# Linear attention and a leaky-ReLU feed-forward on one core: another threading of the first two batches

## The chip, the cores and the metric

The kernel runs on one core of one Trainium2 chip. The metric is device time in microseconds (us) of one execution. The time before is the median of three runs.

Engines are named as in the profile: PE is TensorE's matrix products and PEld its weight loads, DVE is VectorE, ACT is ScalarE, POOL is GpSimd, SP is SyncE, whose queue issues nearly all loads and stores. Each engine, and each queue, works through its instructions in the order of the program.

## The reference

Eight batches of eight heads, 576 positions, head size 64, go through linear attention with cosine and sine weights; the result, reshaped to 4608 rows of 512, goes through a feed-forward of width 2048.

```python
B, H, S, D = q.shape                      # 8, 8, 576, 64
theta = np.pi / 2.0 * pos / S
r = np.maximum(x, 0.0)                    # phi, for q and for k
phi = np.concatenate([r * c, r * s], axis=-1)
kv = np.einsum('bhsf,bhsd->bhfd', k_p, v)
z = np.sum(k_p, axis=2)
num = np.einsum('bhsf,bhfd->bhsd', q_p, kv)
den = np.einsum('bhsf,bhf->bhs', q_p, z)[..., None] + 1e-06
attn = num / den
x = attn.transpose(0, 2, 1, 3).reshape(B * S, H * D)
h = x @ w_in                              # 512 -> 2048
out = np.maximum(0.01 * h, h) @ w_out     # 2048 -> 512
```

## The kernel before

**Groups.** There are nine groups g of 512 rows: one for the first 512 positions of each batch, and a last one for the 64 tail positions of all eight. A group is handled as four tiles j of 128 positions. The order of all instructions is written out by hand; each engine keeps it.

**The stages of a group.** `q_prep` (L300) makes the cosine and sine halves of phi(q) for one tile, in f16 (`phi_half`: on VectorE a tensor_scalar, on ScalarE an activation with Relu). `q_transpose` (L324) turns the eight heads of a tile on TensorE and copies the result `qpT` out of PSUM. `k_main` and `v_main` prepare k and v for a range of heads, on engines named in the call; `k_tail` and `v_tail` do the 64 tail positions. `kv_half` multiplies k and v for four heads, first the two of one pair, then the two of the next, and ScalarE copies the sum out (L291). `num_half` makes numerators and denominators of two tiles and four heads, and `divide` on VectorE forms the quotient in three instructions (L350, L354, L355). `x_transpose_half` turns the quotients and ScalarE copies them into `xT`, the input of the feed-forward. `ffn1` makes two of the 16 blocks of the hidden layer in one PSUM tile (four chunks c of 128 model columns each) and ScalarE applies the leaky ReLU. `ffn2` sums 16 blocks into an output tile, four at a time (`part`), and `ffn2_out` copies it out and stores it.

**Threading.** While the feed-forward products of group g run on TensorE, the attention stages of the next groups are put between them. `weave` takes the units of feed-forward work with a position each, and steps with positions of their own; a step is issued ahead of the first unit at or past its position. Groups 0 and 1 are threaded by hand, ahead of the large weave at the end; from the third batch on `q_steps`, `kv_steps` and `out_steps` place the steps.

**Weights.** w_in comes in eight loads of 512 KB (`load_w1`, two chunks of 128 rows by 512 columns each) and GpSimd casts them to f16 (`cast_w1`). w_out comes in four quarters of 1 MB (`load_w2`) and VectorE casts them (`cast_w2`). `idle(n)` issues n products of zeros on TensorE.

**Loads in order on SP's queue.** First batch: q in two halves of heads, the tails of k and v, then k and v by halves; w_in; then w_out's first two quarters, q of the second batch, its tails, w_out's last two quarters, k and v of the second batch by halves, and q, k, v of the third. Staging tiles rotate through seven buffers.

**PSUM.** Pools "h" and "o" have two buffers each, "n" has one of two banks. A tile of a pool waits until the one that had its buffer before has been read.

Of the kernel before, what the change touches and what calls it, by code (L numbers as in the profile page):

```python
# [18 lines left out]
def kernel(  # L19
# [96 lines left out]
    def load_halves(b):  # L116
# [4 lines left out]

    w1 = [
        [const.tile([P, 2, 512], dt.float16, name=f"w1_{i}_{cp}") for cp in range(2)]
        for i in range(DFF // 512)
    ]
    w2 = const.tile([P, NFT, DM], dt.float16, name="w2")
# [5 lines left out]

    def load_w1(i, cp):

        if cp == 0:
            st["w1", i] = stage.tile([P, NKC, 512], dt.float32, name="w1st", tag="stage")
        sl = slice(2 * cp, 2 * cp + 2)
        nc.sync.dma_start(st["w1", i][:, sl], w1v[:, sl, 512 * i : 512 * (i + 1)])  # L138
# [10 lines left out]
    load_halves(0)  # L149
    for i in range(NB):  # L150
        for cp in range(2):
            load_w1(i, cp)

# [94 lines left out]
    def v_main(b, lo, hi, eng):  # L248
        copy(eng, vmain[b % 2][:, lo:hi, :, 0:D], st["v", b][:, lo:hi])
# [49 lines left out]

    def q_prep(g, j, lo=0, hi=H):  # L300
        src, c, _ = q_src(g, j)
        if lo == 0:
            st["qp", g, j] = qppool.tile([P, H, F], dt.float16, name="qp", tag="qp")
        qp = st["qp", g, j]
        phi_half(DVE, qp[:, lo:hi, 0:D], src[:, lo:hi], cos_t[:, c : c + 1])
        phi_half(DVE, qp[:, lo:hi, D:F], src[:, lo:hi], sin_t[:, c : c + 1])

# [57 lines left out]

    def num_half(g, jp, hg, where):

        if hg == 0:
            st["xp", g, jp] = qppool.tile([P, 2, H, D], dt.float16, name="xp", tag="qp")
        ps = psum(where, [P, 2, 512], dt.float32, "ps_numh")  # L370
        for o in range(2):
            for hh in range(4):
                h = 4 * hg + hh
                nc.tensor.matmul(  # L374
                    ps[:, o, hh * NE : (hh + 1) * NE],
                    lhsT=st["qpT", g, 2 * jp + o][:, h, :],
                    rhs=kv[g][:, h, :],
                )
        divide(ps, st["xp", g, jp][:, :, 4 * hg : 4 * hg + 4, :])

    def x_transpose_half(g, jp, hg, ps=None, out=True):

        if ("xT", g) not in st:
            st["xT", g] = xtpool.tile([P, NKC, MAIN], dt.float16, name="xT")
        xp = st["xp", g, jp]
        if ps is None:
            ps = psum("o", [P, 2, 2 * P], dt.float16, "ps_xth")
        for cc in range(2):
            for o in range(2):
                h = 4 * hg + 2 * cc  # L390
                nc.tensor.transpose(
                    ps[:, cc, o * P : (o + 1) * P], xp[:, o, h : h + 2, :], ident
                )
        if out:
            nc.scalar.copy(
                st["xT", g][:, 2 * hg : 2 * hg + 2, jp * 2 * P : (jp + 1) * 2 * P], ps
            )

# [9 lines left out]
    def ffn1(g, m, lo=0, hi=MAIN, chunks=range(NKC), where="h"):  # L408
# [7 lines left out]
        for c in chunks:  # L416
            nc.tensor.matmul(  # L417
                ps[:, m % 2, lo:hi],
                lhsT=w1[m // 4][c // 2][:, c % 2, m % 4 : 512 : 4],
                rhs=xT[:, c, lo:hi],  # L420
# [63 lines left out]

    def cast_w1(i, cp, eng):
        sl = slice(2 * cp, 2 * cp + 2)
        copy(eng, w1[i][cp], st["w1", i][:, sl])

    def cast_w2(i, eng):
        copy(eng, w2[:, 4 * i : 4 * i + 4, :], st["w2", i])  # L490

    for hg in range(2):
        for j in range(2):
            q_prep(0, j, 4 * hg, 4 * hg + 4)
    for j in range(J):
        if j > 1:
            q_prep(0, j)
        q_transpose(0, j, ACT)  # L500
        idle(1)
    kp_tiles(0)
    k_tail(0, DVE, DVE)
    v_tail(0, DVE)
    for j in range(J):
        k_main(0, j, DVE, DVE, 0, 4)
    v_main(0, 0, 4, ACT)
    for j in range(2):
        k_main(0, j, ACT, DVE, 4, 8)
    idle(6)  # L510
    kv_half(0, 0, "o")
    for j in range(2, J):
        k_main(0, j, DVE, DVE, 4, 8)
    v_main(0, 4, 6, DVE)
    v_main(0, 6, 8, ACT)
    idle(1)
    num_half(0, 0, 0, "n")
    num_half(0, 1, 0, "h")
    idle(3)
    kv_half(0, 1, "o")  # L520
    for i in range(NB):
        for cp in range(2):
            cast_w1(i, cp, POOL)
    x_transpose_half(0, 0, 0)
    num_half(0, 0, 1, "n")
    half = 2 * P
    for m in range(2):
        ffn1(0, m, 0, half, range(0, 2))
    x_transpose_half(0, 1, 0)
    for m in range(2, 4):  # L530
        ffn1(0, m, 0, half, range(0, 2))
    num_half(0, 1, 1, "n")
    x_transpose_half(0, 0, 1)
    for m in range(4):
        ffn1(0, m, half, MAIN, range(0, 2))
    x_transpose_half(0, 1, 1)
    for m in range(4):
        ffn1(0, m, 0, half, range(2, 4))
    for m in range(4):
        ffn1(0, m, half, MAIN, range(2, 4))  # L540

    for i in range(2):
        load_w2(i)
    load_main("q", q, 1)
    load_kvtail("k", k, 1)
    load_kvtail("v", v, 1)
    for i in range(2, 4):
        load_w2(i)
    load_halves(1)
# [31 lines left out]

    for j in range(J):
        q_prep(1, j)
    cast_w2(2, DVE)
    kp_tiles(1)
    k_tail(1, DVE, DVE)
    v_tail(1, DVE)
    cast_w2(3, DVE)
    ps = psum("n", [P, 2, DM], dt.float32, "ps_o")
    for tt in range(2):  # L590
        st["ps_o", 0, 2 + tt] = ps[:, tt]
    steps = []
    for j in range(J):
        at(5 + j, q_transpose, 1, j, ACT, "h")
        at(9, k_main, 1, j, ACT, DVE, 0, 4)
    at(9, v_main, 1, 0, 2, DVE)
    at(9, v_main, 1, 2, 4, ACT)
    order = [(0, 0), (1, 0), (2, 0), (3, 0), (0, 1), (1, 1), (2, 1), (3, 1), (2, 2), (3, 2)]
    weave([(n, f2(0, 4 * tt + part)) for n, (tt, part) in enumerate(order)], steps)
    for tt in (2, 3):  # L600
        ffn2(0, 4 * tt + 3, None)
    ffn2_out(0, 2, DVE)
    ffn2_out(0, 3, DVE)
    ffn2(0, 2)
    kv_half(1, 0, "h", False)
# [5 lines left out]
    v_main(1, 6, 8, ACT)  # L611
    ffn2(0, 4 + 2)
    num_half(1, 0, 0, "h")
    num_half(1, 1, 0, "n")
    ffn2(0, 3, None)
    kv_half(1, 1, "h")
    ffn2_out(0, 0, ACT)
    ffn2_mm(0, 1, 12, 14)
    num_half(1, 0, 1, "h")
    num_half(1, 1, 1, "h")  # L620
    ps = psum("n", [P, 2, MAIN], dt.float16, "ps_x")
    for jp in range(2):
        x_transpose_half(1, jp, 0, ps[:, :, jp * 2 * P : (jp + 1) * 2 * P], False)
    nc.scalar.copy(st["xT", 1][:, 0:2, :], ps)  # L624
    ffn2_mm(0, 1, 14, 16)
    ffn2_out(0, 1, DVE)
    ps = psum("o", [P, 2, 2, 2 * P], dt.float16, "ps_x1")
    x_transpose_half(1, 0, 1, ps[:, 0])
    for m in range(2):
        ffn1(1, m, 0, MAIN, range(0, 2))  # L630
    x_transpose_half(1, 1, 1, ps[:, 1])
    for m in range(2, 4):
        ffn1(1, m, 0, MAIN, range(0, 2))
    for m in range(4):
        ffn1(1, m, 0, MAIN, range(2, 4))
# [3 lines left out]
    units = []  # L639
    for m in range(4, NFT):  # L640
        units.append((8 + m / 2, f1(1, m, "n" if m < 6 else "h")))
    for g in range(1, NG):
# [95 lines left out]
```

## Time and profile before

| | us |
|---|---|
| median of three runs | 295.75 (295.68 to 295.9) |
| the profiled execution, as a whole | 296.48 |
| its span, first instruction to last | 294.7 |
| granted TensorE clock, mean | 1.00 |

Busy time of the engines in stretches of the span, and the mean busy share of the DMA engines:

| stretch, us | PE | DVE | ACT | DMA share |
|---|---|---|---|---|
| 0 to 20 | 16.32 | 15.44 | 11.79 | 0.96 |
| 20 to 30 | 10.00 | 1.23 | 6.62 | 1.04 |
| 30 to 45 | 14.66 | 9.47 | 7.97 | 1.09 |
| 45 to 55 | 9.69 | 9.21 | 5.48 | 1.11 |
| 55 to 70 | 15.00 | 8.94 | 10.78 | 1.15 |
| 70 to 100 | 30.00 | 20.20 | 12.31 | 1.17 |

Matrix products are pipelined and their ends are modelled, so the start of one to the start of the next says what one costs, and a small gap can be hidden in a busy figure. A line of a timeline gives the start and the length in us, the engine, the line of the kernel, the operation, what is written from what, and in brackets the idle time ahead of it with what ended it. The first batch's ramp fills the first 20 us; the feed-forward products of group 0 run until 51, those of group 1 begin there.

### The profile page before, as it was taken

Reading aid. Unit: us, or ns where it says so; the run is one execution under the profiler, and the core shown is the slowest. Engines: PE = TensorE matmul, PEld = TensorE weight load, DVE = VectorE, ACT = ScalarE, POOL = GpSimd, SP = SyncE. Lnnn points to the kernel's source line nnn. Section 1 sums busy time; section 2 is a strip of 40 time slices with the busy share of each in tenths; the row PEclk is TensorE's granted clock in tenths of the full one; section 3 lists DMA queues with packets and bytes.
Section 4 is the critical chain, followed back from the end, with each engine's and each line's share of the span. In section 5 each row is a group of like instructions: output and inputs, shape, how many; then the busy total and the mean of one; then the engine's idle time right before and its main releaser. Section 6 shows DMA issues by size and latency. Waiting matters only on the chain.

```text
span 294.7 us, 4802 instructions
## 1 busy us (share of the span) xinstructions
PE 286.4 (97%) x1932; PEld 153.9 (52%) x1932; DVE 129.9 (44%) x329; ACT 117.9 (40%) x143; POOL 11.0 (4%) x20
## 2 busy tenths in 40 slices
PE   7799999999999999999999999999999999999995
PEld 3585556565465455555545554555445544444444
DVE  6951488945846816823562356233323211000011
ACT  4846366754352722642263226322222232222200
POOL 2064000000000000000000000000000000000000
PEclk9999999999999999999999999999999999999999
DMA  7999999999999999989683997416671211011132
GB/s 222 361 385 406 325 362 331 300 155 336 232 271 325 179 265 335 178 158 332 171 152 82 292 276 148 107 55 145 145 160 51 73 53 38 36 46 60 39 71 71
DMA packets 88773, 56.93 MB, mean 193 GB/s; under 512 B 56880, under 2 KB 81712, under 8 KB 88240
## 3 DMA queue, kind: packets, MB, share of 16 engines
q1 hardware_dynamic: 88672, 56.57, 74.2%
q8 instruction: 15, 0.25, 0.4%
q14 instruction: 6, 0.05, 0.1%
q10 hardware_dynamic: 80, 0.07, 0.1%
HBM read 36.70 MB, written 9.44 MB: 157 GB/s over the span
## 4 chain that ended last, share of the span: by engine, by line
PE 81%; DMA 8%; SPq 6%; ACT 1%; issue 1%; DVE 1%; ACTq 0%
PE ps_h L417 38%; PE ps_o L440 37%; SPq L96 4%; DMA w2st<-in_moe_w_out_dram 4%; DMA w1st<-in_moe_w_in_dram 4%; PE ps_num L339 3%; PE ps_kv L270 2%; SPq L86 1%; DMA out_dram<-osb 1%; SPq L138 1%; ACT vmain L228 1%; SPq L142 1%; PE ps_kv L260 1%; DVE w L230 0%; PE ps_numh L374 0%
## 5 line engine op out<-in xcount | busy, mean ns | idle before, releaser
L417 PE MATMUL ps_h<-xT,w 128*128 128x512 f16 (+1 forms) x592 | 142.6, 373 | 0.3 <-ACT xT L624 0.2
L440 PE MATMUL ps_o<-w,g 128*128 128x512 f16 x560 | 139.5, 379 | 0.3 <-DVE w L230 0.3
L425 ACT ACTIVATE g<-ps_h 128x1024 f16<-128x1024 f32 x72 | 73.5, 1024 | 132.9 <-PE ps_h L417 132.7
L417 PEld LDWEIGHTS <-w 128*128 128x128 f16 x592 | 64.4, 113 | 52.3 <-issue 0.3
L440 PEld LDWEIGHTS <-g 128*128 128x128 f16 x560 | 54.1, 98 | 62.0 <-issue 0.6
L230 DVE COPY osb<-ps_o 128x512 f32<-128x512 f32 x34 | 23.4, 690 | 80.1 <-PE ps_o L440 80.1
L350 DVE TENSOR_SCALAR den<-ps_num 128x8 f32<-128x8 f32 x28 | 4.6, 166 | 52.9 <-PE ps_num L339 52.9
L355 DVE TENSOR_TENSOR xs<-ps_num,rden 128x512 f16<-128x512 f32 x28 | 19.4, 691 | 1.0
L222 DVE TENSOR_SCALAR qp<-qst,cos_t 128x512 f16<-128x512 f32 (+1 forms) x34 | 15.8, 465 | 4.9 <-DMA qst<-in_q_dram 4.9
L222 DVE TENSOR_SCALAR kpm<-kst,sin_t 128x512 f16<-128x512 f32 (+1 forms) x40 | 16.5, 428 | 0.8 <-DMA kst<-in_k_dram 0.8
L222 DVE TENSOR_SCALAR qp<-qst,sin_t 128x512 f16<-128x512 f32 (+1 forms) x34 | 15.8, 465 | 0.0
L339 PEld LDWEIGHTS <-qpT 128*128 128x128 f16 (+1 forms) x256 | 11.2, 101 | 7.3 <-issue 1.7
L222 DVE TENSOR_SCALAR kpm<-kst,cos_t 128x512 f16<-128x512 f32 (+1 forms) x29 | 13.0, 449 | 0.1
L228 ACT CAST vmain<-vst 128x1024 f16<-128x1024 f32 (+1 forms) x14 | 12.9, 953 | 0.4 <-DMA vst<-in_v_dram 0.3
L339 PE MATMUL ps_num<-kv,qpT 128*128 128x66 f16 (+1 forms) x256 | 12.4, 194 | 0.0
L270 PEld LDWEIGHTS <-kpm 128*128 128x128 f16 x256 | 10.5, 97 | 2.6 <-DVE kpm L222 0.7
L228 ACT COPY qpT<-ps_qt 128x1024 f16<-128x1024 f16 x8 | 7.8, 1019 | 7.0 <-PE ps_qt L329 7.0
L162 PE MATMUL ps_idle<-blank 128*128 128x512 f16 x28 | 9.1, 462 | 1.2 <-DVE blank L157 1.2
L230 DVE CAST w<-w2st 128x2048 f16<-128x2048 f32 x4 | 4.9, 1228 | 10.7 <-DMA w2st<-in_moe_w_out_dram 10.7
L230 POOL CAST w<-w1st 128x1024 f16<-128x1024 f32 x8 | 8.3, 1042 | 15.1 <-DMA w1st<-in_moe_w_in_dram 15.0
L270 PE MATMUL ps_kv<-vmain,kpm 128*128 128x66 f16 x192 | 8.1, 193 | 0.0
L354 DVE RECIPROCAL rden<-den 128x8 f32<-128x8 f32 x36 | 7.3, 203 | 1.2
(57 smaller groups left out, 97.1 us busy)
## 6 DMA issues: line engine op xcount, KB each, us to landing
out_dram<-osb SPq DMA_DIRECT2D x32, 256.0 KB, 2.5
qst<-in_q_dram SPq DMA_DIRECT2D x7, 1024.0 KB, 6.5
kst<-in_k_dram SPq DMA_DIRECT2D x6, 1024.0 KB, 8.8
vst<-in_v_dram SPq DMA_DIRECT2D x6, 1024.0 KB, 8.9
w1st<-in_moe_w_in_dram SPq DMA_DIRECT2D x8, 512.0 KB, 11.0
w2st<-in_moe_w_out_dram SPq DMA_DIRECT2D x4, 1024.0 KB, 11.5
kst<-in_k_dram SPq DMA_DIRECT2D x4, 512.0 KB, 8.7
vst<-in_v_dram SPq DMA_DIRECT2D x4, 512.0 KB, 8.7
```

Of the source, the lines that this page charges most:

```text
L96: nc.sync.dma_start(t[o * TAIL : (o + 1) * TAIL], v4[o])
L162: nc.tensor.matmul(ps, lhsT=blank[:, 0:P], rhs=blank)
L222: eng.tensor_scalar(out=o, in0=i, scalar1=0.0, scalar2=col, op0=ALU.max, op1=ALU.mult)
L228: nc.scalar.copy(o, i)
L230: eng.tensor_copy(o, i)
L270: nc.tensor.matmul(ps[:, (2 * cc + o) * NE : (2 * cc + o + 1) * NE], lhsT=kpm[:, h, j, :], rhs=vmain[b % 2][:, h, j, :], start=False, stop ...
L339: nc.tensor.matmul(ps[lo:hi, h // 4, (h % 4) * NE : (h % 4 + 1) * NE], lhsT=qpT[:, h, lo:hi], rhs=kv[b][:, h, :],)
L354: nc.vector.reciprocal(rden, den)
L355: nc.vector.tensor_tensor(out=xs, in0=ps[:, :, 0 : 4 * NE].rearrange("p a (b e) -> p a b e", e=NE)[:, :, :, 0:D], in1=rden.rearrange("p (a ...
L417: nc.tensor.matmul(ps[:, m % 2, lo:hi], lhsT=w1[m // 4][c // 2][:, c % 2, m % 4 : 512 : 4], rhs=xT[:, c, lo:hi], start=(c == 0 and lo == 0 ...
L425: nc.scalar.activation(st["g", g][:, m - 1 : m + 1, :], ps, AF.Lrelu)
L440: nc.tensor.matmul(st["ps_o", g, tt], lhsT=st["g", g][:, m, tt * P : (tt + 1) * P], rhs=w2[:, m, :], start=(m == 0), stop=(m == NFT - 1),)
```

## The change

It touches the first two batches alone.

- q of the first batch: all four tiles are prepared by halves of heads; the fourth tile on ScalarE. The fourth tile's `qpT` is copied by VectorE; the third tile's transposition and the numerators use other PSUM pools. Shares of k and v move between ScalarE, VectorE and GpSimd.
- w_in's first 512 KB are loaded and cast as two pieces of 256 KB, and the first products of `ffn1` use one chunk at a time, between the numerators.
- w_out's third quarter is loaded ahead of the second batch's tails and q; its last quarter is cast in two halves.
- Second batch: on VectorE w_out's third quarter and the tails come before q. `ffn2` of group 0 runs its first three parts for all four tiles; the q transpositions stand behind units 9, 10 and 11 and at the end, and the second batch's k and v behind the last of them. Less of `ffn2` is left between the kv and num products that follow; two output copies move to ScalarE ahead of them; `xT` is copied in four pieces.
- `ffn1` of group 1 starts with the first two chunks of six blocks instead of four; the weave starts two blocks later.

The core of the diff:

```diff
-    for i in range(NB):
-        for cp in range(2):
-            load_w1(i, cp)
+    w1_parts = [(0, 0, 1), (0, 1, 1), (0, 2, 2)]
+    for i in range(1, NB):
+        w1_parts += [(i, 0, 2), (i, 2, 2)]
+    for part in w1_parts:
+        load_w1(*part)
...
     for hg in range(2):
-        for j in range(2):
-            q_prep(0, j, 4 * hg, 4 * hg + 4)
+        for j in range(J):
+            q_prep(0, j, 4 * hg, 4 * hg + 4, ACT if j == 3 else DVE)
+    kp_tiles(0)
+    q_transpose(0, 0, ACT)
+    idle(1)
+    q_transpose(0, 1, ACT)
+    idle(1)
+    k_tail(0, DVE, DVE)
+    v_tail(0, POOL)
+    k_main(0, 0, ACT, DVE, 0, 4)
+    for j in range(1, J):
+        k_main(0, j, DVE, DVE, 0, 4)
+    q_transpose(0, 2, ACT, "n")
+    idle(1)
+    v_main(0, 0, 2, DVE)
+    v_main(0, 2, 4, ACT)
+    q_transpose(0, 3, DVE)
+    idle(9)
+    kv_half(0, 0, "o")
     for j in range(J):
...
+        k_main(0, j, ACT, DVE, 4, 8)
+    num_half(0, 0, 0, "h")
+    num_half(0, 1, 0, "n")
+    v_main(0, 4, 6, ACT)
+    v_main(0, 6, 8, POOL)
     idle(6)
...
+    x_transpose_half(0, 0, 0)
     kv_half(0, 1, "o")
...
+    x_transpose_half(0, 1, 0)
     half = 2 * P
+    ps = psum("h", [P, 2, 512], dt.float32, "ps_numh")
     for m in range(2):
-        ffn1(0, m, 0, half, range(0, 2))
-    x_transpose_half(0, 1, 0)
+        ffn1(0, m, 0, half, range(0, 1))
+    num_half(0, 0, 1, None, ps)
+    num_half(0, 1, 1, "n")
+    for m in range(2):
+        ffn1(0, m, 0, half, range(1, 2))
+    for m in range(2):
+        ffn1(0, m, half, MAIN, range(0, 2))
+    x_transpose_half(0, 0, 1)
     for m in range(2, 4):
         ffn1(0, m, 0, half, range(0, 2))
-    num_half(0, 1, 1, "n")
-    x_transpose_half(0, 0, 1)
-    for m in range(4):
+    for m in range(2):
+        ffn1(0, m, 0, half, range(2, 4))
+    x_transpose_half(0, 1, 1)
+    for m in range(2, 4):
         ffn1(0, m, half, MAIN, range(0, 2))
-    x_transpose_half(0, 1, 1)
-    for m in range(4):
+    for m in range(2, 4):
         ffn1(0, m, 0, half, range(2, 4))
     for m in range(4):
         ffn1(0, m, half, MAIN, range(2, 4))
 
-    for i in range(2):
+    for i in range(3):
         load_w2(i)
-    load_main("q", q, 1)
     load_kvtail("k", k, 1)
     load_kvtail("v", v, 1)
-    for i in range(2, 4):
-        load_w2(i)
+    load_main("q", q, 1)
+    load_w2(3)
     load_halves(1)
...
-    for j in range(J):
-        q_prep(1, j)
     cast_w2(2, DVE)
     kp_tiles(1)
     k_tail(1, DVE, DVE)
     v_tail(1, DVE)
-    cast_w2(3, DVE)
+    for j in range(J):
+        q_prep(1, j)
+    cast_w2(3, DVE, 0, 2)
+    cast_w2(3, DVE, 2, 4)
...
+    for j in range(3):
+        at(9 + j, q_transpose, 1, j, ACT, "h")
+    order = [(tt, part) for part in range(3) for tt in range(J)]
+    weave([(n, f2(0, 4 * tt + part)) for n, (tt, part) in enumerate(order)], steps)
+    q_transpose(1, 3, ACT, "h")
     for j in range(J):
-        at(5 + j, q_transpose, 1, j, ACT, "h")
-        at(9, k_main, 1, j, ACT, DVE, 0, 4)
-    at(9, v_main, 1, 0, 2, DVE)
-    at(9, v_main, 1, 2, 4, ACT)
-    order = [(0, 0), (1, 0), (2, 0), (3, 0), (0, 1), (1, 1), (2, 1), (3, 1), (2, 2), (3, 2)]
-    weave([(n, f2(0, 4 * tt + part)) for n, (tt, part) in enumerate(order)], steps)
+        k_main(1, j, ACT, DVE, 0, 4)
+    v_main(1, 0, 2, DVE)
+    v_main(1, 2, 4, ACT)
     for tt in (2, 3):
         ffn2(0, 4 * tt + 3, None)
     ffn2_out(0, 2, DVE)
     ffn2_out(0, 3, DVE)
-    ffn2(0, 2)
+    ffn2(0, 3, None)
+    ffn2_out(0, 0, ACT)
     kv_half(1, 0, "h", False)
     k_main(1, 0, ACT, DVE, 4, 8)
     kv_half_out(1, 0)
...
-    ffn2(0, 4 + 2)
+    ffn2_mm(0, 1, 12, 14)
     num_half(1, 0, 0, "h")
     num_half(1, 1, 0, "n")
-    ffn2(0, 3, None)
+    ffn2_mm(0, 1, 14, 16)
+    ffn2_out(0, 1, ACT)
     kv_half(1, 1, "h")
-    ffn2_out(0, 0, ACT)
-    ffn2_mm(0, 1, 12, 14)
+    x_transpose_half(1, 0, 0)
+    x_transpose_half(1, 1, 0)
     num_half(1, 0, 1, "h")
-    num_half(1, 1, 1, "h")
...
+    num_half(1, 1, 1, "n")
     for m in range(2):
         ffn1(1, m, 0, MAIN, range(0, 2))
+    x_transpose_half(1, 0, 1)
...
+    x_transpose_half(1, 1, 1)
+    for m in range(4, 6):
+        ffn1(1, m, 0, MAIN, range(0, 2), "n")
+    for m in range(6):
         ffn1(1, m, 0, MAIN, range(2, 4))
...
-    for m in range(4, NFT):
-        units.append((8 + m / 2, f1(1, m, "n" if m < 6 else "h")))
+    for m in range(6, NFT):
+        units.append((8 + m / 2, f1(1, m)))
```

## The prediction

> **What bounds the kernel now.** I read the page first: shares by engine, slices, costly groups.
>
> ```profile
> PE 286.4 (97%) x1932; PEld 153.9 (52%) x1932; DVE 129.9 (44%) x329; ACT 117.9 (40%) x143; POOL 11.0 (4%) x20
> PE   7799999999999999999999999999999999999995
> L417 PE MATMUL ps_h<-xT,w 128*128 128x512 f16 (+1 forms) x592 | 142.6, 373 | 0.3 <-ACT xT L624 0.2
> L440 PE MATMUL ps_o<-w,g 128*128 128x512 f16 x560 | 139.5, 379 | 0.3 <-DVE w L230 0.3
> ```
>
> TensorE is busy 97%; the two products of the second stage hold 282 of 294.7 us and wait 0.6 us. Only the ramp and the places where the second batch is threaded into the first one's products can be changed. So the second view is TensorE's timeline there (start, length, last column the wait).
>
> ```profile
> 19.64 0.40 PE L391 MATMUL ps_xth<-ident,xp 128*128 128x128 f16 x4
> 31.98 4.48 PE L440 MATMUL ps_o<-w,g 128*128 128x512 f16 x20
> 36.30 0.61 PE L329 MATMUL ps_qt<-ident,qp 128*128 128x128 f16 x8
> 36.74 1.03 PE L440 MATMUL ps_o<-w,g 128*128 128x512 f16 x4
> 42.90 2.75 PE L440 MATMUL ps_o<-w,g 128*128 128x512 f16 x12 [0.34 <-DVE w L230]
> 51.33 0.40 PE L391 MATMUL ps_x<-ident,xp 128*128 128x128 f16 x4
> 51.91 1.02 PE L417 MATMUL ps_h<-xT,w 128*128 128x512 f16 x4 [0.18 <-ACT xT L624]
> 60.82 0.42 PE L270 MATMUL ps_kv<-vmain,kpm 128*128 128x66 f16 x8
> ```
>
> From start to start, 20 products of 512 columns take 4.32 us: 0.216 each, 0.864 for four (0.108 each for 256 columns); eight transposes take 0.44, 16 numerator products 0.51 (46.97 to 47.48). Ends are modelled past the issue, so the printed waits are too small: eight products from 40.67 are issued by 42.40 and the next starts at 42.90, a wait of 0.50 for w_out's last quarter. In the same way I find 0.20 before the numerators at 49.69, 0.25 before 51.33 and 0.36 before 51.91: 1.31 us of real waits between 32 and 61.
>
> Third, ScalarE and VectorE in the same stretch.
>
> ```profile
> 36.94 1.01 ACT L228 COPY qpT<-ps_qt 128x1024 f16<-128x1024 f16 x1 [3.74 <-PE ps_qt L329]
> 43.12 1.70 ACT L220 ACTIVATE kpm<-kst,cos_t 128x256 f16<-128x256 f32 x4 [1.19 <-DMA kst<-in_k_dram]
> 44.73 0.60 ACT L228 CAST vmain<-vst 128x512 f16<-128x512 f32 x1
> 46.15 0.51 ACT L220 ACTIVATE kpm<-kst,cos_t 128x256 f16<-128x256 f32 x1 [0.81 <-DMA kst<-in_k_dram]
> 46.56 0.36 ACT L291 CAST kv<-ps_kvh 128x264 f16<-128x264 f32 x1
> 50.15 0.17 DVE L350 TENSOR_SCALAR den<-ps_numh 128x8 f32<-128x8 f32 x1 [0.51 <-PE ps_numh L374]
> 51.62 0.69 DVE L355 TENSOR_TENSOR xp<-ps_numh,rden 128x512 f16<-128x512 f32 x1
> 52.83 0.48 DVE L222 TENSOR_SCALAR qp<-qst,cos_t 128x512 f16<-128x512 f32 x1
> 60.34 0.48 DVE L222 TENSOR_SCALAR kpm<-kst,sin_t 128x512 f16<-128x512 f32 x1
> ```
>
> Two things matter. ScalarE does k's cosines as soon as k lands (43.12), long after its last qpT copy. And VectorE works without a gap from 52.83 to 60.82, the sine that the third batch's kv products need as their fourth operand: TensorE issues that one at 60.91 (60.82 plus three of 0.03), with 0.04 to spare.
>
> Last, the landing of single loads of the second batch (issue, then us to landing): q lands at 18.3 + 16.7 = 35.0, w_out's third quarter at 28.9 + 10.1 = 39.0.
>
> ```profile
> L86 SPq DMA_DIRECT2D qst<-in_q_dram x1: 379/379/379, 18.3 to 18.3; - x1
> DMA to landing us min/median/max: 16.7/16.7/16.7
> L142 SPq DMA_DIRECT2D w2st<-in_moe_w_out_dram x1: 1660/1660/1660, 28.9 to 28.9; - x1
> DMA to landing us min/median/max: 10.1/10.1/10.1
> ```
>
> Others read so: first batch's second halves of k 12.7, of v 14.1; w_in pieces 15.5, 16.8, 18.2; w_out's second quarter 30.3, last 41.6; tails 35.7 to 36.7; second batch's k halves 43.1 and 46.1, v halves 44.6 and 47.7. The DMA share is about 1 until 58 us: loads land in issue order at the rate of their bytes.
>
> **First batch: about -0.05.** ScalarE's four q activations (0.51 each, 0.41 apart as at 46.15) lie in its idle 2.30 us before 7.27; without that cover 1.6. The qpT copy on VectorE has no row; 0.69 (128x512 f32 out of PSUM) to 1.38 (twice that) bound it, 1.2 taken, and it hides before k's second half; late next would be the first divide. GpSimd's v tail and v quarter (0.62, its row) fit before w_in. Splitting w_in's first chunks brings 256 KB at 14.8 instead of 15.5, its cast half of 1.04. But the ramp hangs on k and v: sines on VectorE 12.72 to 13.79 (four, 0.267 apart), quotients 1.12 and 1.04 more, 14.9 and 15.95 (15.69 and 16.73 before). ScalarE now does four cosines, not two: 12.72 to 14.36, then its part of v, 14.98 (14.76 before). Second kv half 15.2 (15.09), its copy done 16.40, numerators 16.45 (16.34), VectorE 16.91 to 19.08 (19.58). TensorE gets the third set of transposes at 18.08, the copy ends 19.11, products waiting for it run to 19.59, and the fourth set starts at 19.60 against 19.64. Behind it stand the same 16 short and 48 long products. The earlier quotients go into other waits; ffn2 starts at 31.93. I allow 0.3 either way.
>
> **The load order: about 0.** w_out's third quarter, the tails and then q follow the 30.3 landing. The bytes ahead of the last quarter are the same, so it stays at 41.6 and k and v stay; q is now last of its set, 39.0 if all else is equal. Lower bound 2.6 (quarter) + 1.75 (q to last tail before) + 2.95 (next q behind its predecessor) after 30.3: 37.6. Upper 39.5. I take 38.8, nearest the equal-bytes row. VectorE's two halves of a q tile end 0.95 after landing (34.96 to 35.85, then a semaphore), 39.75; TensorE arrives after nine groups of four, 31.93 + 7.78 = 39.71. Stall 0.04. One more load on SP's queue costs one issue (0.7), hidden by loads still in flight.
>
> The Trainium skill, "DMA: Bandwidth & Descriptors", section "Anatomy of one DMA — SWDGE (gpsimd) path", gives each DMA a fixed 2.0 us besides its bytes; paid in line, one more load would put the sum at about 299. The trace disagrees for this queue: w_in's 512 KB pieces land 1.3 to 1.4 us apart, and 64 KB tails 0.2 to 0.45 apart.
>
> **w_out's last quarter: -0.50.** It is used eight products later (1.73) and cast in two halves (each half of 1.23): ready 42.7, after q's four tiles end on VectorE (42.0), needed 44.1. The wait goes.
>
> **The second batch: the loss.** Call Q the start of the fourth q transposition: 31.93 + 12 x 0.864 + 3 x 0.44 + 0.04 = 43.66. Before, it was 40.23 and k's cosines came 2.9 us later; now they stand behind its copy on ScalarE. Times after Q: copy 0.64 (36.30 to 36.94), next instruction +0.92, four cosines +1.61, part of v +0.50, the osb copy moved here +0.50, one cosine +0.41: kv copy at 4.58, done 4.94. Numerators at 4.99; TensorE had reached there at 4.5 after waiting 0.14 and 0.29 in the kv half. Quotients: first den +0.46, second pair's xp +2.16 more: 7.61. TensorE, done with the second kv half at 6.6, transposes at 6.8 and waits 0.86 to 7.66, numerators 7.88, ffn1 after the xT copy 8.73 (0.34). All four tiles divided at 10.50; TensorE issues third-batch kv products from 17.81 if alone: 0.7 us later than 60.77. VectorE takes the next q at 10.42 and needs 7.99 (52.83 to 60.82): 18.41, so the fourth product is issued at 18.46, where TensorE alone is at 17.95. Before it was 60.91: the shift is 43.66 + 18.46 - 60.91 = **+1.21**. By waits: 1.31 removed, 2.2 added in the second batch, 0.5 before the third batch's kv: about +1.3 with the rest, the same to 0.1. After that the order is unchanged and TensorE is full. The profiled execution has a span of 294.7 and took 296.48; what lies around the span (1.8) stays, so it becomes 297.7. The median of the three runs is 0.73 below that execution, and so I say **297.0**.
>
> **Rivals.**
> - The q load lands at 39.5 or the ramp is 0.5 slower: Q moves by up to 0.7, +1.9, 297.7. For it, q's landing was 4.65 behind its predecessor, not 2.95. Against, the tails slowed it then.
> - VectorE's part is hidden and ScalarE's shorter: +0.3 to +0.7, 296.1 to 296.45. It needs the third batch's sines by 17.9.
> - Other side: the queue on ScalarE is no wait. If the kv copy ends by Q + 3.5 (47.2), fillers cover the second batch; then -1.31 - 0.05: 294.4. It decides where the cosines start: right behind k's landing or behind the copy. For it, TensorE had no wait at 45.48 before; against, ScalarE keeps program order and its queue sums to 4.94.
> - Nothing changes (ramp and threading both masked): 295.75.
> - Each load costs a fixed time in line: by the tails' 0.45 at most, +1.6, 297.4; the rule of that DMA page is this one with 2.0.
>
> **Chances.** Forecast (+0.9 to +1.6) 0.56; late q 0.14; hidden part 0.13; other side 0.13; nothing 0.02; fixed cost per load 0.02. 0.2% (0.59 us) is about what can be told from no change. Faster 0.13; same takes nothing and most of the hidden part, 0.14; slower 0.73. The range goes from 295.6 to 298.1, leaving out most of the other side and q beyond 39.9; the forecast's own is 296.6 to 297.4.
>
> **What would show it.** The fourth set of first-batch transposes near 19.6 and ffn2 near 31.9; no wait on w_out; the first q transposition near 39.8; kpm cosines on ScalarE directly behind a qpT copy, near 45.2; kv copy near 48.2; waits of TensorE for xp near 51; the third batch's sine ending near 62.1. Wrong if ffn2 starts before 31, or the cosines run at 43.1.

## The result and the profile after

| | us |
|---|---|
| before, median of 6 runs on the same chip | 295.87 (295.68 to 295.91) |
| after, median of 6 runs | 297.27 (297.15 to 297.48) |
| ratio, with its 95% interval | 1.005 (1.0037 to 1.0063) |
| the profiled execution of after / its span | 297.15 / 295.4 |

The changed kernel is 1.40 us slower. Forecast were 297.0, and 296.6 to 297.4 for the likeliest case alone. Medians and ratios here and below leave out the one execution at a much lower granted TensorE clock, one of e_v_late (337.05 us, 0.852).

The page of the kernel after, its first part and the groups of products (busy us and mean ns of one, then the idle time ahead of them):

```profile
span 295.4 us, 4824 instructions
...
PE 287.2 (97%) x1936; PEld 154.3 (52%) x1936; DVE 128.8 (44%) x325; ACT 119.7 (41%) x151; POOL 12.7 (4%) x24
...
L428 PE MATMUL ps_h<-xT,w 128*128 128x512 f16 (+1 forms) x592 | 142.9, 373 | 0.4 <-ACT xT L405 0.4
L451 PE MATMUL ps_o<-w,g 128*128 128x512 f16 x560 | 139.0, 379 | 0.0
...
L276 PE MATMUL ps_kv<-vmain,kpm 128*128 128x66 f16 x192 | 8.3, 193 | 0.4 <-DVE kpm L228 0.4
```

TensorE still sets the time. `ps_o` no longer waits for `w`; in its place `ps_kv` waits for `kpm`, the sines of the third batch. By shares of busy time the two kernels look alike: the loss is 1.4 us of 296 and has to be read from the timeline.

TensorE's timeline after the change:

```profile
19.11 0.39 PE L397 MATMUL ps_xth<-ident,xp 128*128 128x128 f16 x4
...
31.44 7.93 PE L451 MATMUL ps_o<-w,g 128*128 128x512 f16 x36
39.21 0.61 PE L335 MATMUL ps_qt<-ident,qp 128*128 128x128 f16 x8
...
43.14 0.61 PE L335 MATMUL ps_qt<-ident,qp 128*128 128x128 f16 x8
43.59 2.75 PE L451 MATMUL ps_o<-w,g 128*128 128x512 f16 x12
...
48.17 0.67 PE L381 MATMUL ps_numh<-kv,qpT 128*128 128x66 f16 x16 [0.31 <-ACT kv L297]
...
50.84 0.40 PE L397 MATMUL ps_xth<-ident,xp 128*128 128x128 f16 x4 [0.64 <-ACT xT L405]
...
51.91 1.02 PE L428 MATMUL ps_h<-xT,w 128*128 128x512 f16 x4 [0.16 <-ACT xT L405]
...
61.66 0.33 PE L276 MATMUL ps_kv<-vmain,kpm 128*128 128x66 f16 x5 [0.36 <-DVE kpm L228]
...
62.77 1.03 PE L428 MATMUL ps_h<-xT,w 128*128 128x512 f16 x4
```

From 31.44 to the q transpositions there is no wait (31.44 + 36 x 0.216 = 39.22). The waits come after the fourth one at 43.14, in the numerators, the transposes, `ffn1` and the third batch's kv. What they wait for first is ScalarE's queue. Its timeline in the same execution:

```profile
43.84 1.01 ACT L234 COPY qpT<-ps_qt 128x1024 f16<-128x1024 f16 x1 [0.30 <-PE ps_qt L335]
44.75 1.70 ACT L226 ACTIVATE kpm<-kst,cos_t 128x256 f16<-128x256 f32 x4
46.35 0.60 ACT L234 CAST vmain<-vst 128x512 f16<-128x512 f32 x1
46.86 0.58 ACT L234 COPY osb<-ps_o 128x512 f32<-128x512 f32 x1
47.34 0.51 ACT L226 ACTIVATE kpm<-kst,cos_t 128x256 f16<-128x256 f32 x1
47.75 0.36 ACT L297 CAST kv<-ps_kvh 128x264 f16<-128x264 f32 x1
```

No idle time stands between the qpT copy and the kv copy: each instruction starts behind the one before it, and the kv copy comes 4.61 us after the fourth q transposition. VectorE's timeline, three of its lines (the q of the second batch, the q of the third, and the sine for the fourth product of the third batch's kv):

```profile
38.20 0.49 DVE L228 TENSOR_SCALAR qp<-qst,cos_t 128x512 f16<-128x512 f32 x1 [2.19 <-DMA qst<-in_q_dram]
...
53.61 0.48 DVE L228 TENSOR_SCALAR qp<-qst,cos_t 128x512 f16<-128x512 f32 x1
...
61.12 0.48 DVE L228 TENSOR_SCALAR kpm<-kst,sin_t 128x512 f16<-128x512 f32 x1
```

VectorE begins the third batch at 53.61 and is at its last sine from 61.12 on, without a gap; TensorE's fourth kv product follows at 61.66.

### The profile page after: what moved, and what is told of

The parts are those of the page before. It is cut to its first block, busy times and chain, and to the rows that moved or that the text cites. A ratio compares the mean times of both kernels' runs of the same rounds, so it can differ in the third digit from the quotient of the medians.

```text
span 295.4 us, 4824 instructions
## 1 busy us (share of the span) xinstructions
PE 287.2 (97%) x1936; PEld 154.3 (52%) x1936; DVE 128.8 (44%) x325; ACT 119.7 (41%) x151; POOL 12.7 (4%) x24
## 4 chain that ended last, share of the span: by engine, by line
PE 87%; DVE 4%; ACT 4%; DMA 2%; issue 1%; SPq 0%; ACTq 0%; DVEq 0%
PE ps_h L428 39%; PE ps_o L451 39%; PE ps_num L345 3%; PE ps_kv L276 2%; DVE qp L228 2%; PE ps_idle L168 1%; DMA qst<-in_q_dram 1%; PE ps_qt L335 1%; ACT vmain L234 1%; ACT kpm L226 1%; DVE kpm L228 1%; DMA out_dram<-osb 1%; DVE xp L361 1%; PE ps_xth L397 1%; ACT xT L405 1%
## 5 line engine op out<-in xcount | busy, mean ns | idle before, releaser
L236 DVE COPY osb<-ps_o 128x512 f32<-128x512 f32 x33 | 22.7, 691 | 81.6 <-PE ps_o L451 81.6
L228 DVE TENSOR_SCALAR kpm<-kst,cos_t 128x512 f16<-128x512 f32 (+1 forms) x26 | 11.9, 458 | 0.0
L168 PE MATMUL ps_idle<-blank 128*128 128x512 f16 x32 | 9.7, 447 | 1.2 <-DVE blank L163 1.2
L236 DVE CAST w<-w2st 128x2048 f16<-128x2048 f32 (+1 forms) x5 | 5.0, 1009 | 12.7 <-DMA w2st<-in_moe_w_out_dram 12.7
L234 ACT COPY qpT<-ps_qt 128x1024 f16<-128x1024 f16 x7 | 7.0, 1013 | 8.3 <-PE ps_qt L335 8.3
L236 POOL CAST w<-w1st 128x1024 f16<-128x1024 f32 (+1 forms) x9 | 8.5, 948 | 3.3 <-DMA w1st<-in_moe_w_in_dram 3.3
```

What stands on the lines that cost most here:

```text
L168: nc.tensor.matmul(ps, lhsT=blank[:, 0:P], rhs=blank)
L228: eng.tensor_scalar(out=o, in0=i, scalar1=0.0, scalar2=col, op0=ALU.max, op1=ALU.mult)
L234: nc.scalar.copy(o, i)
L236: eng.tensor_copy(o, i)
```

## The experiments

The runs are in three sets, each on another chip: the first four below, then e_v_pool to e_split, then the rest. The kernel before ran beside each set on its chip, and the ratios are against that; they are estimates from all runs together and not quotients of the medians (which differ most in e_order). The kernel after was measured apart from them, so differences from its 297.27 are not of one set; the kernel before has 295.67 to 295.87 on the four occasions.

| run | median us | ratio (95%) | median span | profiled span |
|---|---|---|---|---|
| before, beside the three sets | 295.67, 295.73, 295.76 | | 293.9, 293.9, 294.0 | |
| e_before | 295.69 | 1.0002 (0.9993 to 1.0010) | 293.9 | 293.8 |
| e_first | 295.97 | 1.0013 (1.0005 to 1.0022) | 293.9 | 294.0 |
| e_second | 297.36 | 1.0058 (1.0045 to 1.0071) | 295.6 | 295.4 |
| e_cos_dve | 296.77 | 1.0039 (1.0027 to 1.0051) | 295.0 | 295.0 |
| e_v_pool | 298.15 | 1.0077 (1.0063 to 1.0092) | 296.3 | 296.3 |
| e_both | 298.08 | 1.0081 (1.0067 to 1.0095) | 296.3 | 296.3 |
| e_best | 297.96 | 1.0073 (1.0059 to 1.0087) | 296.2 | 296.3 |
| e_split | 295.52 | 0.9995 (0.9986 to 1.0003) | 293.7 | 293.7 |
| e_v_late | 297.00 | 1.0047 (1.0035 to 1.0059) | 294.9 | not comparable |
| e_three | 296.32 | 1.0026 (1.0017 to 1.0034) | 294.5 | 294.5 |
| e_old_plus | 296.10 | 1.0013 (1.0003 to 1.0023) | 294.3 | 294.5 |
| e_order | 299.96 | 1.0126 (1.0101 to 1.0151) | 298.2 | 296.5 |

The kernel after has a median span of 295.45 (295.4 to 295.7 in its six runs). Time less span is about 1.8 us, in the median, in all kernels but two: in e_first and e_v_late it is 2.1.

### e_before: the kernel before, profiled a second time

No edit. The execution shown before took 296.48, 0.73 above its median, so its waits are read here in another execution.

> The kernel before, unchanged, for a second trace. Its first trace came from an execution of 296.48, 0.73 above the median, and the comparison of the two traces shows only 0.7 of the 1.4 us lost. Theory: the ramp of that execution was late, because k's second half landed at 12.7 there and at 12.2 in the trace of the changed kernel: here ffn2 starts at 31.4 to 31.6 and the span is near 294.1. Rival: the ramp is 31.98 again, and the 0.7 lies behind 62 us, in the part both kernels share. Time 295.9 by both.

This one took 295.58, with a span of 293.8, and `ffn2` starts at 31.65, 0.33 earlier than in the first trace, where 31.4 to 31.6 were expected. TensorE's timeline:

```profile
31.65 4.48 PE L440 MATMUL ps_o<-w,g 128*128 128x512 f16 x20
...
39.90 0.61 PE L329 MATMUL ps_qt<-ident,qp 128*128 128x128 f16 x8
40.34 4.48 PE L440 MATMUL ps_o<-w,g 128*128 128x512 f16 x20
44.66 0.22 PE L260 MATMUL ps_kvh<-vtail,kpt 128*128 128x132 f16 x1
...
46.14 0.67 PE L374 MATMUL ps_numh<-kv,qpT 128*128 128x66 f16 x16
...
50.99 1.02 PE L417 MATMUL ps_h<-xT,w 128*128 128x512 f16 x4 [0.18 <-ACT xT L624]
...
61.09 1.03 PE L417 MATMUL ps_h<-xT,w 128*128 128x512 f16 x4
```

ScalarE's, in the same execution:

```profile
41.54 1.71 ACT L220 ACTIVATE kpm<-kst,cos_t 128x256 f16<-128x256 f32 x4
...
44.55 0.51 ACT L220 ACTIVATE kpm<-kst,cos_t 128x256 f16<-128x256 f32 x1 [0.79 <-DMA kst<-in_k_dram]
45.48 0.38 ACT L291 CAST kv<-ps_kvh 128x264 f16<-128x264 f32 x1 [0.42 <-PE ps_kvh L270]
```

And one line of VectorE's:

```profile
41.54 1.14 DVE L222 TENSOR_SCALAR kpm<-kst,sin_t 128x256 f16<-128x256 f32 x4 [0.29 <-DMA kst<-in_k_dram]
```

Two things follow. First, the wait of 0.50 for w_out's last quarter is not there: 20 products run through from 40.34 to 44.66 (20 x 0.216 = 4.32). Second, the cosines start 1.64 after the transposition at 39.90 (1.61 after the one at 43.14 in the changed kernel). Here the end of the qpT copy and the landing of k fall together: VectorE's sines, which wait for k, start at 41.54 as well. In the program of the kernel before, the same cosines stand behind the same copy; what the change adds to ScalarE's queue ahead of the kv copy is one osb copy (0.5). But 20 products stand between the last q transposition and the kv products, where after the change there are 12, and four between the kv products and the numerators, where there are two. So here the kv copy waits for TensorE, and not TensorE for the kv copy: ScalarE is done with the cosine at 44.55, which had waited for k's second half, before the kv products are.

This trace, from an execution near the median, is what the others are compared with below.

### e_first and e_second: the two parts alone

e_first is the kernel after with the load order, the second batch and the start of `ffn1` of group 1 as before:

```diff
-    for i in range(3):
+    for i in range(2):
         load_w2(i)
+    load_main("q", q, 1)
     load_kvtail("k", k, 1)
     load_kvtail("v", v, 1)
-    load_main("q", q, 1)
-    load_w2(3)
+    for i in range(2, 4):
+        load_w2(i)
...
-        at(9 + j, q_transpose, 1, j, ACT, "h")
+        at(5 + j, q_transpose, 1, j, ACT, "h")
...
```

e_second is the kernel before with just these as in the kernel after.

> The first batch's part alone (ScalarE's share of q, PSUM pools, w_in's first pieces apart, order of the ramp); load order of w_out and q and the second batch as before. Theory (the loss is all in the second batch, the ramp hangs on k and v): 295.6 to 296.0, no more than 0.3 either way; fourth set of first-batch transposes within 0.2 of the kernel before. Rival (the ramp's part costs too, or one more load on the queue costs a fixed time): 296.4 or more. Rival (the ramp part is a gain that the second batch eats): 295.3 or less.

> The second batch's part and the load order alone; the ramp and w_in's loads as before. Theory: 297.1 to 297.5, as the changed kernel; kv copy of the second batch 4.6 to 4.9 behind the start of the fourth q transposition. Rival (half of the loss is the ramp's): 296.4 to 296.7.

e_second costs 1.69 us (297.36 against 295.67); its first `ffn2` product starts at 31.44, its span is 295.4, and the times of its second batch on TensorE and ScalarE are those of the kernel after to 0.01. The loss is in the second batch and the load order. The two medians add up to 1.99, more than the 1.40 of the whole change; by the median spans the parts add 0 and 1.7 to 293.9, and the kernel after has 295.45. e_first is 0.30 slower than before by its time and equal by its median span (293.9 both): taken as a whole, the first batch's part gains and loses nothing inside the span, and the 0.30 lies around it. What it is there, no trace shows. Its profiled execution has a wait that e_before's has not. A line of TensorE and one of VectorE:

```profile
40.24 4.75 PE L447 MATMUL ps_o<-w,g 128*128 128x512 f16 x20
```

```profile
40.95 1.23 DVE L236 CAST w<-w2st 128x2048 f16<-128x2048 f32 x1 [0.36 <-DMA w2st<-in_moe_w_out_dram]
```

The 20 products take until 44.82 instead of 44.56: w_out's last quarter came 0.92 later than in e_before (cast from 40.95 and 40.03), and TensorE waits 0.26 for it. In the first profiled execution of the kernel before it landed at 41.6, 1.57 later than the cast in e_before began. The wait predicted as removed exists in some executions and not in others, as the same load lands. Why it lands earlier or later was not tried.

### e_split: w_in's first 512 KB as two pieces, nothing else

```diff
-    for i in range(NB):
-        for cp in range(2):
-            load_w1(i, cp)
+    w1_parts = [(0, 0, 1), (0, 1, 1), (0, 2, 2)]
+    for i in range(1, NB):
+        w1_parts += [(i, 0, 2), (i, 2, 2)]
+    for part in w1_parts:
+        load_w1(*part)
```

> The kernel before with w_in's first 512 KB loaded and cast as two pieces, nothing else changed. The first batch's part alone took 295.97 against 295.67. Theory (a further load costs nothing in line; those 0.3 come from the ramp's part or from when loads land): 295.5 to 295.8. Rival (a fixed cost for one more load puts w_out's last quarter later, TensorE waits for it): 295.9 to 296.1, w_out's last cast 0.3 or more later than 40.0.

295.52 against 295.73: one more load on SP's queue costs nothing that can be measured, and w_out's last cast starts at 40.36, between e_before's 40.03 and e_first's 40.95. The rival of a fixed cost for each load in line falls. The Trainium skill ("DMA: Bandwidth & Descriptors", section "Anatomy of one DMA — SWDGE (gpsimd) path") gives a DMA on the gpsimd path about 2.0 us besides its bytes and puts most of it down to completion latency; this run shows no such cost for a further load on SP's queue, behind others in flight.

### e_order: the load order alone

```diff
-    for i in range(2):
+    for i in range(3):
         load_w2(i)
-    load_main("q", q, 1)
     load_kvtail("k", k, 1)
     load_kvtail("v", v, 1)
-    for i in range(2, 4):
-        load_w2(i)
+    load_main("q", q, 1)
+    load_w2(3)
```

> The kernel before with only the load order changed: w_out's third quarter ahead of the second batch's tails and q. Theory: q lands near 38, TensorE reaches the first q transposition at 36.0 and waits to 38.9, w_out's third and last quarters are cast behind q's tiles on VectorE; 2.5 to 3.5 slower, 298.2 to 299.2. Rival (loads land when they are needed anyway): within 0.3.

299.96 in the median, 298.29 in the profiled execution: slower by 4.2 and by 2.5, where 2.5 to 3.5 were expected. TensorE's timeline in that execution has nearly all of its price in one line:

```profile
38.67 0.62 PE L329 MATMUL ps_qt<-ident,qp 128*128 128x128 f16 x8 [2.22 <-DVE qp L222]
```

The q transposition behind 20 products waits for q, which VectorE prepares from 37.73 on, 4.02 later than in e_before (33.71). So the moved q transpositions of the change are what the load order asks for, and in the kernel after they meet q without a wait; the transpositions moved alone were not run. The rest of the median goes with the clock: four of the six runs, at 299.81 to 300.29, have a mean granted TensorE clock of 0.994, the two at 297.91 and 298.29 of 0.998 and 1.0. 0.6% of 298 is 1.8 us, about what they differ by. That the clock is the cause is not shown: no trace of those runs was kept.

### e_cos_dve: the second batch's first four cosines on VectorE

```diff
     for j in range(J):
-        k_main(1, j, ACT, DVE, 0, 4)
+        k_main(1, j, DVE, DVE, 0, 4)
```

> The changed kernel with the second batch's first four cosines on VectorE, which idles there 1.3 us, instead of on ScalarE behind the last qpT copy. Theory (ScalarE's queue behind the fourth q transposition is the wait): the kv copy is then held only by the output copy ahead of it, which waits for TensorE at 46.2; numerators 0.7 earlier (47.5 for 48.17), all behind it too, 296.6. Rival (the queue is no wait; the loss is TensorE's order or the late q): within 0.2 of the changed kernel, 297.1 to 297.4.

296.77, 0.50 under the kernel after. One line of ScalarE's timeline, then two of TensorE's:

```profile
47.22 0.37 ACT L297 CAST kv<-ps_kvh 128x264 f16<-128x264 f32 x1
```

```profile
47.64 0.67 PE L381 MATMUL ps_numh<-kv,qpT 128*128 128x66 f16 x16 [0.30 <-ACT kv L297]
...
61.31 0.33 PE L276 MATMUL ps_kv<-vmain,kpm 128*128 128x66 f16 x5 [0.35 <-DVE kpm L228]
```

Counted from the last q transposition (43.09 here, 43.14 after), the kv copy starts at 4.13 instead of 4.61, the numerators at 4.55 instead of 5.03, and the third batch's fourth kv product at 18.22 instead of 18.52. Taking work off ScalarE's queue moved everything behind it: that the queue is the wait is shown. It gives no more because the osb copy on ScalarE still stands in front (it waits for TensorE's product until 46.33), and the second wait, at the third batch's kv, stays as long as it was (0.52).

### e_v_pool, e_both, e_best: the third batch's v on GpSimd

GpSimd has nothing to do from 48 on, so v of the third batch was moved there from VectorE, whose queue the third batch's kv waits for:

```diff
-    kv_steps(2, 9.7, 0.5, 13, DVE, 2)
+    kv_steps(2, 9.7, 0.5, 13, POOL, 2)
```

e_both adds the edit of e_cos_dve, and e_best moves the osb copy of the first tile behind the kv copy as well:

```diff
-    ffn2_out(0, 0, ACT)
     kv_half(1, 0, "h", False)
     k_main(1, 0, ACT, DVE, 4, 8)
     kv_half_out(1, 0)
+    ffn2_out(0, 0, ACT)
```

> The changed kernel with the third batch's v (two casts of 1024 columns, two tail casts) on GpSimd, which idles then, instead of VectorE. Theory (VectorE's work ahead of the third batch's fourth kv product is 0.5 of the loss): VectorE's last sine ends 1.8 earlier, TensorE no longer waits at 61.1, 296.7 to 296.9. Rival (that wait is covered by something behind it): 297.1 to 297.4.

> Both repairs on the changed kernel: the second batch's first four cosines on VectorE (alone 296.77), and the third batch's v on GpSimd. Theory (they are two waits in a row, the gains add): 296.1 to 296.4. Rival (one wait seen twice): 296.6 to 296.8.

> As the one with both repairs, and ScalarE's output copy of tile 0 set behind the second batch's kv copy instead of ahead of it. Theory: the kv copy then waits for the kv products alone (0.3 earlier than with the cosines on VectorE), numerators and all behind them 0.3 earlier: 295.8 to 296.1. Rival (the quotients on VectorE, 2.16 for a pair, bound the rest whatever ScalarE does): same as with both repairs, 296.1 to 296.4.

All three missed: 298.15, 298.08 and 297.96, slower than the kernel after. Of e_v_pool, a line of GpSimd's timeline, one of VectorE's and one of TensorE's:

```profile
56.42 4.10 POOL L236 CAST vmain<-vst 128x1024 f16<-128x1024 f32 x1 [9.37 <-DMA vst<-in_v_dram]
```

```profile
59.14 0.48 DVE L228 TENSOR_SCALAR kpm<-kst,sin_t 128x512 f16<-128x512 f32 x1
```

```profile
62.36 0.22 PE L266 MATMUL ps_kv<-vtail,kpt 128*128 128x132 f16 x1 [1.34 <-POOL vtail L236]
```

And the groups of e_v_pool's GpSimd by shape:

```profile
L236 POOL CAST w<-w1st 128x1024 f16<-128x1024 f32 x7 | 7.3, 1043 | 3.6 <-DMA w1st<-in_moe_w_in_dram 3.6
L236 POOL CAST vmain<-vst 128x1024 f16<-128x1024 f32 x2 | 5.1, 2567 | 9.4 <-DMA vst<-in_v_dram 9.4
```

The theory was right about VectorE: its last sine of the third batch ends at 59.62, 1.98 earlier than after the change (61.60). But the same cast of 128x1024 that takes 1.04 for w_in took 4.10 while VectorE worked through its tensor_scalars (from its start to that of the next cast, 60.47, it is 4.05). It ends 0.90 behind VectorE's last one (60.52 and 59.62); in e_both and e_best the distance is 0.90 and 0.89 too. So nearly all of the 1.04 seems to be done after VectorE stops. The second cast and the tails follow, and TensorE waits until 62.36. The Trainium skill ("SBUF — State Buffer", section "Who interferes with whom") says that GpSimd's only port pair is VectorE's second one, and that where a VectorE instruction runs in a mode that takes both pairs, as a tensor_scalar can, whoever issues first holds the pair for the whole instruction and the other is blocked fully. These three traces agree with it; which mode VectorE was in, they do not show.

e_best's own edit shows in its trace all the same: there the kv copy starts 3.86 after the last q transposition (47.42 and 43.56), the numerators have no printed wait, and `ffn1` starts at 8.17 (8.48 in e_cos_dve, 8.77 after). All three have a span of 296.3, whatever came before: GpSimd's cast sets the end.

### e_v_late and e_three: v behind the sines, and three repairs together

e_v_late leaves v on VectorE, but the second half of the third batch's v comes behind the last sine:

```diff
-        at(start + 3 * step + 0.1, v_main, b, 4, 8, eng_v)
+        at(start + (4.1 if b == 2 else 3) * step + 0.1, v_main, b, 4, 8, eng_v)
```

e_three is this with the edits of e_cos_dve and of e_best's osb copy.

> The changed kernel with the third batch's second v cast set behind k's last cosine and sine on VectorE (nothing moved to another engine; GpSimd had made it worse, 298.15, since its first cast took 4.1 instead of 1.0 beside VectorE's work). TensorE needs that cast only for the last 16 of 32 products, 0.6 after the first. Theory (VectorE's last sine is 0.5 of the loss): the wait at 61.1 goes, 296.7 to 296.9. Rival (no part of the loss): 297.1 to 297.4.

> Three repairs on the changed kernel: the second batch's first cosines on VectorE, the output copy of tile 0 behind the kv copy, the third batch's second v cast late. Theory (three waits in a row that add): 0.5 + 0.3 + 0.5 below 297.3, 295.9 to 296.1; what is left over the kernel before is the wait for quotients behind the second kv products. Rival (the late q transpositions bound the second batch whatever stands behind): 296.5 or more.

e_v_late: 297.00, 0.27 under the kernel after, where 0.37 to 0.57 were expected. By the median span, 294.9 against 295.45, it gained what the wait at the third batch's kv amounts to; 0.3 more than in the other kernels lies around the span. It has no timeline that can be compared. e_three: 296.32, 0.95 under the kernel after and 0.56 over the kernel before; 295.9 to 296.1 were expected. TensorE's timeline of e_three, and a line of VectorE's:

```profile
47.34 0.67 PE L381 MATMUL ps_numh<-kv,qpT 128*128 128x66 f16 x16
...
50.51 0.40 PE L397 MATMUL ps_xth<-ident,xp 128*128 128x128 f16 x4 [0.64 <-ACT xT L405]
...
60.66 0.22 PE L266 MATMUL ps_kv<-vtail,kpt 128*128 128x132 f16 x1
...
61.90 1.03 PE L428 MATMUL ps_h<-xT,w 128*128 128x512 f16 x4
```

```profile
48.30 0.15 DVE L356 TENSOR_SCALAR den<-ps_numh 128x8 f32<-128x8 f32 x1
```

The third batch's kv runs from 60.66 to 61.90 without the wait, so the late cast does take it away; the numerators' printed wait is gone, and 0.20 by starts are left. What is left besides is 0.57 in or behind the second kv half and 0.82 ahead of the second pair's transposes. Both sets of transposes need quotients: VectorE finishes k's sines at about 48.3 here and only then begins to divide, 0.96 after the numerators' start, so that the first pair's quotients end at 49.41 and its transposes start at 49.47.

### e_old_plus: parts of the change in the kernel before

The kernel before with w_in split as in e_split, w_out's last quarter cast in two halves, and `xT` of the second batch copied in two pieces:

```diff
-    cast_w2(3, DVE)
+    cast_w2(3, DVE, 0, 2)
+    cast_w2(3, DVE, 2, 4)
...
-        x_transpose_half(1, jp, 0, ps[:, :, jp * 2 * P : (jp + 1) * 2 * P], False)
-    nc.scalar.copy(st["xT", 1][:, 0:2, :], ps)
+        x_transpose_half(1, jp, 0, ps[:, :, jp * 2 * P : (jp + 1) * 2 * P])
```

> A version meant to beat both: the kernel before with w_in's first piece split, w_out's last quarter cast in two halves, and the second batch's xT copied in two pieces instead of one of 1.01. Theory: 0.1 to 0.3 below the kernel before, 295.3 to 295.6. Rival (each is hidden): same as the kernel before within 0.1.

It missed: 296.10, 0.34 slower than before, and 0.3 by the median span. TensorE's timeline:

```profile
32.08 4.48 PE L446 MATMUL ps_o<-w,g 128*128 128x512 f16 x20
...
50.77 0.38 PE L397 MATMUL ps_x<-ident,xp 128*128 128x128 f16 x4 [0.67 <-ACT xT L401]
50.99 0.59 PE L446 MATMUL ps_o<-w,g 128*128 128x512 f16 x2
```

With one copy for both pieces, both transposes follow each other and two `ffn2` products stand behind them. With two, the second transposes wait for the first copy, 0.84 by starts, ahead of those products. Of the 0.84 by which this trace is late at the third batch (61.93 against 61.09), 0.41 are waits in the second batch (1.23 against 0.82) and 0.43 came with the ramp (32.08 against 31.65).

## Why the prediction was right, and where it was wrong

**All waits of TensorE on one table.** From a group's start to the next, less what was issued: 0.216 for a product of 512, 0.22 for four transposes, 0.51 for 16 numerator products, 0.62 for a kv half (44.66 to 45.28 in e_before).

| wait of TensorE ahead of, us | e_before | after | e_cos_dve | e_three |
|---|---|---|---|---|
| or within the first kv half | 0 | 0.48 | 0 | 0 |
| numerators of the first heads | 0 | 0.47 | 0.45 | 0.20 |
| or within the second kv half | 0 | 0.09 | 0.26 | 0.57 |
| numerators of the second heads | 0.20 | 0 | 0 | 0 |
| transposes of the second pair | 0.26 | 0.81 | 0.81 | 0.82 |
| first products of `ffn1` | 0.36 | 0.33 | 0.33 | 0.33 |
| third batch's fourth kv product | 0 | 0.52 | 0.52 | 0 |
| sum | 0.82 | 2.70 | 2.37 | 1.92 |
| first `ffn2` product | 31.65 | 31.44 | 31.39 | 31.35 |
| first product behind the third batch's kv | 61.09 | 62.77 | 62.42 | 61.90 |
| span | 293.8 | 295.4 | 295.0 | 294.5 |

The sums explain the traces. Waits 1.88 longer and a start 0.21 earlier make 1.67; the third batch's kv is left 1.68 later and the span is 1.6 longer. From there to the end each of these traces takes 232.6 to 232.7, so nothing is lost or won in the large weave.

**The second batch** was the heart of the forecast, and it came out to a few hundredths. All after the start of the fourth q transposition:

| | predicted | measured |
|---|---|---|
| qpT copy | 0.64 | 0.70 |
| kv copy | 4.58 | 4.61 |
| numerators | 4.99 | 5.03 |
| transposes of the second pair | 7.66 | 7.70 |
| first `ffn1` products | 8.73 | 8.77 |
| VectorE at the next q | 10.42 | 10.47 |
| third batch's fourth kv product | 18.46 | 18.52 |

Four cosines, part of v, an osb copy and one more cosine stand in ScalarE's program ahead of the kv copy; e_cos_dve shows that fewer of them bring everything forward, and e_three that more can be had in the same way. The 2.2 + 0.5 us of added waits were measured as 2.70.

**Why the queue waits now.** The prediction put it down to cosines that started as soon as k landed and now stand behind a copy. In the program they stand behind that copy in both kernels. In the first trace k landed at 43.1, long after the copy; in e_before it landed just as the copy was done, so that the cosines came 1.64 after the last q transposition, as after the change, and TensorE had no wait there all the same. What the change takes away is cover: 24 `ffn2` products stood between the last q transposition and the numerators, now 14 do, and the osb copy of 0.5 is added to the queue. This is read from the two traces and the program; the cover alone was not varied. The prediction's times were right because it added up the queue, not because of that comparison.

**The start of it** came 0.5 earlier than forecast: predicted 43.66, measured 43.14. Two terms are in that. The first batch was sized at -0.05 with 0.3 either way: `ffn2` starts at 31.44, 0.54 ahead of the first trace but 0.21 ahead of e_before, and e_first's median span says that this part alone is worth nothing that lasts. Over the profiled executions `ffn2` starts at 31.44 to 32.08 with the ramp as before (six of them) and at 31.30 to 31.86 with the new one (seven): each spreads by about 0.6, and the middle of the second lies 0.4 earlier. So the new ramp may gain some tenths, but what is an execution's own is larger, and in e_first's trace the wait of 0.26 for w_out is more than the 0.11 by which `ffn2` starts ahead of e_before. And the stall of 0.04 for q is none: q came early enough (VectorE starts on it at 38.20, within 37.6 to 39.5 as estimated, 0.6 ahead of the value taken). e_order shows the other side of that step: with the transpositions where they were, the moved q would have cost 2.15 us (e_order's fastest run, 297.91) or more.

**The mis-sized term** is w_out's last quarter, -0.50. That wait was real in the trace it was read from, and is 0 in e_before and 0.26 in e_first's trace. Of the 1.31 us of waits to be removed only 0.82 are there in an execution near the median. The term was also counted twice. The first trace's span is 0.9 longer than e_before's, of which 0.49 are these waits and 0.33 the later start of `ffn2`; so the wait was part of what lay above the median. The prediction took it off as a gain of the change and then took off the 0.73 by which that execution exceeded its median, too. Without it the sum would have been about 1.7; measured are 1.40, and 1.69 in e_second. Against the first trace, with its 296.48, the execution after is only 0.67 longer. That a forecast half a microsecond too low in this term still came within 0.27 is in part luck: the kernel after came out 0.3 lower against its own kernel before than e_second did against its.

**The rivals.** "The q load is late" did not come up: no wait ahead of 39.21. "VectorE's part is hidden" fell on the wait of 0.52 at the third batch's kv. "The queue is no wait" needed the kv copy by 3.5 after the last q transposition: it came at 4.61 (e_best, with the osb copy out of the way, has it at 3.86). "A fixed cost for each load" fell with e_split, for one more load of 256 KB. "Nothing changes" is excluded by the interval of the ratio.

**What stays open.** What the 0.3 us around the span of e_first and e_v_late are; why loads land up to 1.6 us apart in executions of one kernel; what the cover alone is worth. No kernel tried is faster than the one before: e_split equals it, and the three repairs of e_three leave the change 0.56 behind, with the quotients still waited for.

## What to carry to other kernels

When a step is moved later past filler work, add up the serial queue behind it (here 4.6 us on ScalarE) and compare it with the filler that is left (14 products instead of 24), engine by engine; that sum was good to 0.06 us. Read a wait in two executions before it is counted as a gain. An execution that is longer than its median may be so because of the very wait that is to be removed: then the wait must not be counted besides. An idle GpSimd was no free helper here, beside a VectorE that worked without gaps: look at such a cast beside such work before moving more there.

## What the runs showed of the hardware that was not expected

- A GpSimd cast of 128x1024 from f32 to f16 took 4.10, 3.95 and 3.77 us beside VectorE's tensor_scalars, and 1.04 without them. The other way, three sines on VectorE took 1.22 instead of 0.87 where a GpSimd cast of 128x512 began 0.12 after them (46.72 and 46.84, kernel after).
- Four of e_order's six runs had a granted TensorE clock of 0.994; the runs of the kernel after have 0.999 to 1.0. Those four take 1.5 us and more above the other two. e_order is the only kernel here in which TensorE stands still for over 2 us among the products (2.4 by starts, ahead of 38.67); whether that is the cause was not tried.
- What lies around the span is the same to 0.1 us in eleven kernels and 0.3 us more in two, so that a median of times can differ by what no part of the timeline shows.
- The same load, w_out's last quarter in the kernel before, was there at 41.6 in one execution and by 40.03 in another. It makes or removes a wait of 0.5 us, while the medians of the kernel before on four occasions lie within 0.20 (295.67 to 295.87).
